# A third pre-mix input tile, clearing in parts, and one copy for both post-mix banks

## The chip, the cores and the metric

One core of one Trainium2 chip runs the kernel. The metric is the device time of one execution in microseconds. Three runs of the kernel before took 1095.16, 1096.00 and 1097.95 us; the median is 1096.0 us.

## The reference

```python
scores = scale * q @ k.transpose                      # 4 batches, 12 heads, 448 x 448, head dim 64
scores = einsum('bhij,hg->bgij', scores, w_pre)       # mix over heads before the softmax
attn   = exp(scores - max) / (sum + 1e-9)             # softmax over j
attn   = einsum('bhij,hg->bgij', attn, w_post)        # mix over heads after it
x      = attn @ v                                     # -> 1792 tokens x 768
x      = elu(x @ w_in) @ w_out                        # 768 -> 2048 -> 768
h      = x @ w_in2                                    # 768 -> 1024
h      = layernorm(h * softmax(h)) * g_ln
out    = h @ w_out2                                   # 1024 -> 768
```

Queries and keys are fp32, and so is all the attention arithmetic. The weights of the two feed-forward layers come as float64 and are decoded on the chip into pairs of high and low parts.

## The kernel before

**Tiling of the attention.** The 448 query rows of a batch are cut into groups of 10 rows. Groups are gathered into 17 chunks (`CH`, line 25) of 4, 8, 12, 12, 9 groups in batch 0, then 11, 12, 12, 10; 12, 12, 12, 9; and 11, 12, 12, 10. For a chunk the scores of all 12 heads are computed with the query rows on the partitions (line 443, tile `sc`, six operations of two heads each), copied out of PSUM by ScalarE or VectorE (line 449, tiles `sev`), and moved by DMA (line 455 to 460, issued through line 400) into one tile `sp` with (row, head) on the partitions and the groups on the free axis. Each head's move goes to 10 partitions, one per row of a group; head 11 takes two moves, so that a chunk has 13 moves.

**Units.** Two neighbouring groups make a unit; there are 90, numbered 0 to 89, and chunk 13 begins with unit 67, chunk 14 with unit 73. For each unit TensorE does the pre-mix (line 510, `pm<-sp,wpre_t`), VectorE takes two maxima (515), ScalarE two exponentials with their sums (520), VectorE guards and inverts the sums (524, 527), GpSimd scales the post-mix weights (531), and TensorE does the post-mix (543), which writes one PSUM bank for each of the unit's two groups (`po_p`, two tiles, line 136). Each bank is then copied into the tile `at` by one instruction (551, 128x480, or 128x384 where a group is cut at 448 rows). When a chunk's copies are done, two operations `av` (592) multiply with `v`; the result is copied (599) and stored.

**What sets the order.** Nothing here is written in the order in which it runs. `op` (290) records an operation with a rank, its dependences, its engines with assumed costs, and the ring buffers it takes and uses; `schedule` (296) then places all of them, engine by engine, by those costs and emits each engine's instructions in that order. An engine runs its instructions strictly in the emitted order, and the DMA issues on SP, ScalarE and GpSimd stand in these orders too. An operation that may run on two engines (evacuations, copies, moves of the first chunks) gets the one on which it ends first by the assumed costs.

**The tile `sp`.** There are two of them (pools `spa` and `spb`, lines 129 and 403 ff.); chunk c uses the tile of chunk c-2 (line 453). The moves of chunk c can therefore start only after the last pre-mix of chunk c-2. Both are cleared whole at the start (lines 468 to 470), one by VectorE and one by GpSimd, because the moves leave partitions unwritten. The 8 tiles `sev`, the ring of `k` (12 tiles, two batches), the three `sc` banks, three `pm` banks and two `po` banks are the other rings. Scores of a chunk are ranked from the first pre-mix of the chunk before to `SCM` = 12 us ahead of its own first pre-mix (line 398 ff.).

**Behind the attention** come the two feed-forward layers (from about 373 us of the span on), which the change does not touch, except that the pools freed at line 664 have another name among them.

Of the kernel before, what the change touches and what calls it, by code (L numbers as in the profile page):

```python
# [9 lines left out]
F32 = mybir.dt.float32  # L10
# [4 lines left out]
ALU = mybir.AluOpType  # L15
# [3 lines left out]
NB, NH, S, D = 4, 12, 448, 64  # L19
# [18 lines left out]
XB = 2  # L38
# [12 lines left out]
DB = .9  # L51
DA = .2
T0 = 14
SCM = 12
KD = 3.5
VD = 28
WB = 3
SB = 8
VB = 2
EB = 10  # L60
LEAD = 3

@with_exitstack
def kernel(ctx: ExitStack, tc: tile.TileContext, qa, kt, vt, wpre, wpost,
# [8 lines left out]
    def pool(name, bufs=1, side="left", space=None):  # L73
        kw = {"space": space} if space is not None else {"side": side}
        p = tc.alloc_tile_pool(name=name, bufs=bufs, reuse_waits="tile", **kw)
        pools[name] = p
        return p

    def release(*names):
        for n in names:  # L80
            pools.pop(n).release()
# [45 lines left out]
    wpost_t = const.tile([128, 60], F32, name="wpost_t")  # L127

    pool("spa", 1, "right")
    k_p = pool("k", 12, "right")  # L130
    kst_p = pool("kst", 2, "right")
    q_p = pool("q", 4, "right")
    sev_p = pool("sev", SB, "right")

    ps_sc = pool("ps_sc", 3, space=PSUM)
    ps_po = pool("ps_po", 1, space=PSUM)
    po_p = [ps_po.tile([128, 512], F32, name=f"po{i}") for i in range(2)]
    ps_pm = pool("ps_pm", 3, space=PSUM)


# [6 lines left out]
    def width_of(c):  # L147
        return min(10 * CH[c][2], S - CH[c][1])
# [130 lines left out]
    class Op:  # L279
# [2 lines left out]
    ops = []  # L282
    tail = {"pe": .3, "act": .2, "dve": .17, "pool": .1, "sp": 2.0, "host": 0.0}
    bufs = {"sc": 3, "pm": 3, "po": 2, "sev": SB, "e": EB, "wr": WB, "st": 4, "kst": 2, "q": 4,
            "k": 12, "sp0": 1, "sp1": 1, "at": 2, "v": VB, "x": XB, "ws": 4, "wy": 2}

    def op(rank, emit, deps=(), new=(), uses=(), more=0.0, lag=None, **us):

        o = Op()
        o.rank, o.emit, o.deps, o.new, o.us, o.more, o.lag = rank, emit, [d for d in deps if d is not None], new, us, more, lag  # L290
        for b in chain(new, uses):
            b.users.append(o)
        ops.append(o)
        return o

    def schedule():
        free = dict.fromkeys(tail, 0.0)
        rings = {r: [] for r in bufs}
        todo = sorted(ops, key=lambda o: o.rank)

        def seen(o, e):

            if o.lag is not None:
                return o.end + o.lag
            if o.eng == e and e not in ("sp", "dve"):
                return o.end
            return o.end + tail[o.eng] + o.more

        def ready(o, e):
            t = 0.0  # L310
            for d in o.deps:
                if d.end is None:
                    return None
                t = max(t, seen(d, e))
            more = dict.fromkeys(bufs, 0)
            for b in o.new:
                ring = rings[b.ring]
                n = bufs[b.ring] - more[b.ring]
                more[b.ring] += 1
                if b.at is None and len(ring) >= n:  # L320
                    for u in ring[-n].users:
                        if u.end is None:
                            return None
                        t = max(t, seen(u, e))
            return t

        while todo:
            cand, start = [], {}
            for o in todo[:WIN]:
                opts = []  # L330
                for e, us in o.us.items():
                    r = ready(o, e)
                    if r is None:
                        break
                    r = max(r, o.rank - (AHS if e == "sp" else AHD))
                    opts.append((max(r, free[e]) + us + (DB if e == "dve" and "pool" in o.us and o.rank > TD else DA if e == "dve" and "act" in o.us else 0.0), r, e))
                else:
                    _, r, e = min(opts)
                    cand.append((o, e, r))
                    start[e] = min(start.get(e, 1e9), max(r, free[e]))  # L340
            e = min(start, key=start.get)
            o, _, r = min((c for c in cand if c[1] == e and c[2] <= start[e] + GRACE), key=lambda c: c[0].rank)
            o.eng = e
            t = max(r, free[e])
            o.end = free[e] = t + o.us[e]
            for b in o.new:
                if b.at is None:
                    b.at = o
                    rings[b.ring].append(b)
            o.emit(e)  # L350
            todo.remove(o)
        return max(free.values())
# [3 lines left out]
    def copier(e):  # L356
        return nc.scalar.copy if e == "act" else nc.vector.tensor_copy
# [41 lines left out]
    def dma(out, in_, e="sp"):  # L399
        {"act": nc.scalar, "pool": nc.gpsimd, "sp": nc.sync}[e].dma_start(out=out, in_=in_)  # L400
# [27 lines left out]
    def add_score(c, h):  # L428

        b, _, G = CH[c]  # L430
        n = 5 * G
        ring = ("sc", "pm")[h // 2 % 2] if c == 0 else "sc"
        scb, svb = [Buf(ring) for _ in range(2)], [Buf("sev") for _ in range(2)]
        r = t_sc[c, h]
        key = "sc", c, h

        def mm(e):
            T[key] = [pools["ps_" + ring].tile([128, 512], F32, tag=ring, name="sc") for _ in range(2)]
            q, k = q_t[c, h // 6], kt_t[b, h]
            for x in range(2):  # L440
                for i in range(2):
                    sl = slice(64 * i, 64 * i + 64)
                    nc.tensor.matmul(T[key][i][64 * x:64 * x + 64, :S], q[sl, h % 6 // 2, 64 * x:64 * x + 64], k[sl, :],  # L443
                                     start=True, stop=True)

        def evac(e, i):
            t = T["sv", c, h + i] = (k0.tile([128, S], F32, name=f"s0_{h + i}") if c == 0 else
                                     sev_p.tile([128, S], F32, tag="sev", name="sev"))
            copier(e)(t, T[key][i][:, :S])  # L449

        def move(e, i, p, r0, r1):
            if c not in sp_t:
                sp_t[c] = sp_t[c - 2]
            dma(sp_t[c][p:p + 13 * (r1 - r0 - 1) + 1:13, 0:G, :], T["sv", c, h + i][r0 * G:r1 * G], e)

        o1 = op(r, mm, [k_op[b, h], q_op[c, h // 6]], scb, [qb_[c, h // 6], kb[b, h]], pe=SC)
        for i in range(2):
            sv = [] if c == 0 else [svb[i]]
            o2 = sc_ev[c, h + i] = op(r + .9 + .1 * i, lambda e, i=i: evac(e, i), [o1], sv, [scb[i]], act=.43, dve=.54)
            for n, to in enumerate([(h + i, 0, 10)] if h + i < 11 else [(11, 0, 5), (64, 5, 10)]):  # L460
                sp_op.setdefault(c, []).append(op(r + 2 + .2 * i + .1 * n, lambda e, i=i, to=to: move(e, i, *to), [o2], [spb_[c]], sv, lag=3.5, sp=.78, **({"act": .78} if c < 2 else {"pool": 1.0} if c == 2 else {})))

    spb_ = {c: Buf(f"sp{(NC - c) % 2}") for c in range(NC)}
    o = op(7.0, lambda e: dma(wpre_t, wpre), sp=.5)
    o_wpost = op(T0 + 2, lambda e: dma(wpost_t, wpost), sp=.5)
    w_op = op(T0 - 8, lambda e: nc.gpsimd.tensor_scalar(wpre_t, wpre_t, 0.125, None, ALU.mult), [o], pool=.6)

    for c in range(2):
        sp_t[c] = pools["spb" if (NC - c) % 2 else "spa"].tile([128, NH, S], F32, tag="sp", name="sp")
        (nc.gpsimd if c else nc.vector).memset(sp_t[c], 0.0)  # L470
    for t in po_p:
        nc.vector.memset(t, 0.0)

    def begin(e):
        release("k0")
# [21 lines left out]
    for u, sl in enumerate(units):  # L497
# [46 lines left out]
                                         wr_t[u][sl, r].rearrange("p (g a) -> p g a", a=5), start=True, stop=True)  # L544

        def take(e, s, u=u, sl=sl):
            c, g = sl[s]
            if c not in at_t:
                at_t[c] = pools["at"].tile([128, 4, NH, WMAX], F32, tag="at", name="at")
            o, n = 10 * g, min(10, width_of(c) - 10 * g)  # L550
            copier(e)(at_t[c].rearrange("p q h r -> p (q h) r")[:, :, o:o + n],
                      po_t[u][s][:, :480].rearrange("p (x a) -> p x a", a=10)[:, :, :n])

# [8 lines left out]
        ow = op(r0 + 3.4, weigh, [o, o_wpost], [wb], [sb], dve=.3, pool=.38)  # L562
        r0 = t_post[u]
        o = op(r0, post, ex + [ow], pob, eb + [wb], pe=POST)
        for s, (c, g) in enumerate(sl):
            at_ops[c].append(op(r0 + 1.2 + .1 * s, lambda e, s=s, take=take: take(e, s), [o], [at_b[c]] if g == 0 else [],
                                [pob[s]] + ([at_b[c]] if g else []), act=.45, dve=.57))
# [93 lines left out]

    def start_moe(e):
        nonlocal gln_t
        release("sev", "q", "kst", "k", "spa")
        p = pool("wstg", 2, "right")
        gln_t = p.tile([128, F2 // 128], F32, name="gln_t", bufs=1)
        dma(gln_t, gln)
        w1_alloc(0, pool("w1a", 1, "right"))
        xT_alloc(0, pool("xT0", 1, "right"))
# [302 lines left out]
```

## Time and profile before

| | |
|---|---|
| median of 3 runs | 1096.0 us (1095.16 to 1097.95) |
| the profiled execution | 1094.9 us, of which the span of its instructions is 1093.1 us |
| busy share of the span | TensorE 97%, VectorE 66%, ScalarE 46%, GpSimd 21% |
| first pre-mix starts, last `av` ends | 17.85 us, 373.5 us |

Times below are from the span's start. A matmul's end is modelled, so the busy share of TensorE says little on how tightly it works; the chain of waits and the start of one operation against the next say more. The program records each matmul of the attention as two, so that one score or pre-mix operation is 8 records, a post-mix 56, an `av` 48.

### The profile page before, as it was taken

To read this page: it belongs to the slowest core of one execution; us is meant where nothing else is said; L and a number is where in the kernel's file an instruction comes from. 1 tells how busy PE (TensorE), PEld (TensorE's weight loads), DVE (VectorE), ACT (ScalarE), POOL (GpSimd) and SP (SyncE) were. 2 spreads that over 40 slices of the span, in tenths; PEclk is the share of its full clock that TensorE was granted. 3 is DMA by queue.
4 is the path that set the end of the run, shared out by engine and by line. 5 is a ranking of instruction groups with operands and counts; after the bars stand their busy time and mean duration, and the time that the engine had idled before them with its cause. 6 is when DMAs were issued, how large, how long until landed. Compare 5 with 4: busy or idle time off the path is not lost.

```text
span 1093.1 us, 28427 instructions
## 1 busy us (share of the span) xinstructions
PE 1059.9 (97%) x11800; PEld 888.6 (81%) x11800; DVE 722.0 (66%) x1391; ACT 504.2 (46%) x1071; POOL 231.6 (21%) x243
## 2 busy tenths in 40 slices
PE   6899999999999999999999999999999999999998
PEld 2457667667666898998988999999999889898988
DVE  6576687677677557687887887878864644353522
ACT  3566676677676455333333443333431434342422
POOL 2211010011011325343343433343431000000000
PEclk9999999999999999999999999999999999999999
DMA  6875775775746442415234242423262400000001
GB/s 200 210 209 172 216 238 172 219 221 176 232 149 197 132 133 72 155 58 171 99 117 149 83 154 77 140 91 126 70 243 100 194 30 15 30 23 22 30 15 44
DMA packets 80287, 141.69 MB, mean 130 GB/s; under 512 B 20853, under 2 KB 59969, under 8 KB 80157
## 3 DMA queue, kind: packets, MB, share of 16 engines
q1 hardware_dynamic: 78345, 136.59, 39.1%
q10 hardware_dynamic: 1332, 2.09, 0.6%
q8 instruction: 93, 1.52, 0.6%
q0 software_dynamic: 480, 1.19, 0.4%
q14 instruction: 37, 0.30, 0.1%
HBM read 75.96 MB, written 25.17 MB: 93 GB/s over the span
## 4 chain that ended last, share of the span: by engine, by line
PE 74%; DMA 9%; DVE 8%; ACT 4%; issue 2%; SPq 1%; POOL 1%; ACTq 0%; DVEq 0%; POOLq 0%
PE h L256 15%; PE o L745 15%; PE o L888 11%; PE h L841 11%; PE av L592 6%; PE sc L443 5%; PE pm L510 5%; PE po L543 5%; DMA sp<-sev 3%; DMA ws<-in_wo_dram 2%; DVE x L761 1%; DVE wy L184 1%; DMA ws<-in_wi_dram 1%; PE tr L872 1%; DVE wq L180 1%
## 5 line engine op out<-in xcount | busy, mean ns | idle before, releaser
L520 ACT ACTIVATE e<-pm,st 128x448 f32<-128x448 f32 x180 | 113.4, 635 | 72.3 <-DVE st L515 65.9
L515 DVE TENSOR_REDUCE st<-pm 128x1 f32<-128x448 f32 x180 | 105.1, 617 | 60.9 <-PE pm L510 58.6
L745 PE MATMUL o<-gh,woh 128*128 128x448 f32 x384 | 141.3, 368 | 3.8 <-ACT x L759 1.9
L745 PE MATMUL o<-glo,woh 128*128 128x448 f32 x384 | 139.9, 364 | 0.0
L745 PE MATMUL o<-gh,wol 128*128 128x448 f32 x384 | 139.8, 364 | 0.0
L443 PE MATMUL sc<-kt,q 64*64 64x448 f32 x816 | 123.8, 565 | 9.7 <-ACT sev L449 4.6
L543 PEld LDWEIGHTS po<-wr,e 60*64 60x64 f32 x5040 | 102.4, 135 | 37.0 <-issue 23.8
L269 POOL TENSOR_TENSOR glo<-g,gh 128x448 fp32r<-128x448 f32 x64 | 83.1, 1298 | 217.9 <-issue 124.5
L510 PE MATMUL pm<-sp,wpre_t 64*64 64x448 f32 x720 | 112.2, 558 | 10.4 <-DMA xs<-x 4.4
L888 PE MATMUL o<-w,lh 128*128 128x384 f32 x448 | 120.3, 340 | 0.0
L543 PE MATMUL po<-wr,e 60*64 60x60 f32 x5040 | 109.1, 219 | 2.3 <-issue 1.1
L841 PE MATMUL h<-w,x2h 128*128 128x512 f32 x336 | 107.7, 395 | 0.0
L761 DVE TENSOR_TENSOR x<-x,o 128x448 f32<-128x448 f32 x168 | 101.4, 610 | 7.9 <-PE o L745 7.9
L256 PE MATMUL h<-xh,wih 128*128 128x448 f32 x288 | 105.5, 366 | 0.0
L256 PE MATMUL h<-xh,wil 128*128 128x448 f32 x288 | 105.0, 365 | 0.0
L256 PE MATMUL h<-xl,wih 128*128 128x448 f32 x288 | 104.9, 364 | 0.0
L264 ACT ACTIVATE t<-t 128x448 f32<-128x448 f32 x64 | 37.0, 578 | 134.7 <-DVE t L263 134.7
L531 POOL TENSOR_TENSOR wr<-wpost_t,st 128x120 f32<-128x120 f32 x90 | 36.3, 403 | 294.7 <-DVE st L527 225.7
L592 PEld LDWEIGHTS av<-at,v 128*64 128x64 f32 x1632 | 75.8, 137 | 14.1 <-DVE st L515 3.5
L592 PE MATMUL av<-at,v 128*64 128x120 f32 (+5 forms) x1632 | 83.2, 258 | 3.3 <-issue 1.8
L745 PEld LDWEIGHTS o<-gh,woh 128*128 128x128 f32 x384 | 72.1, 188 | 12.7 <-DVE x L761 4.5
L888 PEld LDWEIGHTS o<-w,lh 128*128 128x128 f32 x448 | 81.7, 188 | 0.6
(98 smaller groups left out, 1930.2 us busy)
## 6 DMA issues: line engine op xcount, KB each, us to landing
sp<-sev SPq DMA_DIRECT2D x94, 210.0 KB
ws<-in_wi_dram SPq DMA_DIRECT2D x33, 512.0 KB
ws<-in_wo_dram SPq DMA_DIRECT2D x21, 512.0 KB
q<-in_qa_dram SPq DMA_DIRECT2D x34, 192.0 KB
v<-in_vt_dram SPq DMA_DIRECT2D x24, 256.0 KB
w2s<-ws SPq DMA_DIRECT2D x12, 512.0 KB
ws<-in_wo_dram SPq DMA_DIRECT2D x16, 384.0 KB
w2s<-ws SPq DMA_DIRECT2D x16, 384.0 KB
```

The source lines that it names most:

```text
L256: nc.tensor.matmul(ps[:, :S], a[:, kc * FG + ft * 128:kc * FG + (ft + 1) * 128], x[:, kc, :], start=kc == 0 and n == 0, stop=kc == ECH - 1 ...
L269: nc.gpsimd.tensor_tensor(glo, g, f(gh), ALU.subtract)
L443: nc.tensor.matmul(T[key][i][64 * x:64 * x + 64, :S], q[sl, h % 6 // 2, 64 * x:64 * x + 64], k[sl, :], start=True, stop=True)
L510: nc.tensor.matmul(ps_t[u][r][64 * s:64 * s + 64, :S], wpre_t[p, :], sp_t[c][p, g, :], start=True, stop=True)
L515: nc.vector.tensor_reduce(out=st_t[u][:P, r:r + 1], in_=ps_t[u][r][:P, :S], op=ALU.max, axis=AX.X, negate=True)
L520: nc.scalar.activation(out=t[:P], in_=ps_t[u][r][:P, :S], func=AF.Exp, bias=st[:P, r:r + 1], scale=1.0, accum_out=st[:P, 2 + r:3 + r])
L543: nc.tensor.matmul(out[:, :, 5 * r:5 * r + 5], e_t[u, r][sl, 64 * n:64 * n + 64], wr_t[u][sl, r].rearrange("p (g a) -> p g a", a=5), start ...
L592: nc.tensor.matmul(ps[64 * k:64 * k + 64, i, :], v_t[CH[c][0]][:, 6 * n + 2 * i + k, q, :], at_t[c][:, q, 6 * n + 2 * i + k, :w], start=q ...
L745: nc.tensor.matmul(ps[:, :S], a[:, ft * DM + e * 128:ft * DM + (e + 1) * 128], x, start=n == 0, stop=n == 5)
L761: nc.vector.tensor_tensor(x1[tb][:, e, :], x1[tb][:, e, :], ps[:, :S], ALU.add)
L841: nc.tensor.matmul(ps[:, hf * 512:hf * 512 + 512], a[:, k, :], w, start=n == 0, stop=n == 3 * ECH - 1)
L888: nc.tensor.matmul(ps[:, :384], a[:, k, :], w, start=n == 0, stop=n == 3 * FC - 1)
```

## The change

There are now three `sp` tiles (pool `spc`), chunk c uses that of chunk c-3, and the ring of `k` shrinks from 12 to 8 tiles to make room. At the start the tile of chunk 0 is cleared only in its 4 groups (by VectorE), that of chunk 1 in its 8 groups and that of chunk 2 whole (by GpSimd); the rest of the first two is cleared later by GpSimd, before chunks 3 and 4 need it. Moves of chunk 2 may now be issued by ScalarE or SP, not by GpSimd. The scaling of `wpre_t` goes from GpSimd to VectorE, and the clearing of the two `po` banks gets a place in the schedule. The two banks become one tile of two banks, and where both groups of a unit belong to one chunk and are whole, one instruction of 128x2x48x10 copies both. Assumed numbers of the scheduler change: `SCM` 12 to 15, the landing of a move 3.5 to 5.0 us for chunks from 2 on, and the times from which VectorE and GpSimd are free.

```diff
-SCM = 12
+SCM = 15
+KB = 8
     pool("spa", 1, "right")
-    k_p = pool("k", 12, "right")
+    pool("spc", 1, "right")
+    k_p = pool("k", KB, "right")
-    po_p = [ps_po.tile([128, 512], F32, name=f"po{i}") for i in range(2)]
+    po_2 = ps_po.tile([128, 2, 512], F32, name="po")
+    po_p = [po_2[:, i] for i in range(2)]
+        free["pool"], free["dve"] = 8.0, 3.5
-                sp_t[c] = sp_t[c - 2]
+                sp_t[c] = sp_t[c - 3]
-                sp_op.setdefault(c, []).append(op(r + 2 + .2 * i + .1 * n, lambda e, i=i, to=to: move(e, i, *to), [o2], [spb_[c]], sv, lag=3.5, sp=.78, **({"act": .78} if c < 2 else {"pool": 1.0} if c == 2 else {})))
-    spb_ = {c: Buf(f"sp{(NC - c) % 2}") for c in range(NC)}
+                sp_op.setdefault(c, []).append(op(r + 2 + .2 * i + .1 * n, lambda e, i=i, to=to: move(e, i, *to), [o2, o_clear.get(c)], [spb_[c]], sv, lag=3.5 if c < 2 else 5.0, sp=.78, **({"act": .78} if c < 3 else {})))
+    spb_ = {c: Buf(f"sp{(NC - c) % 3}") for c in range(NC)}
-    w_op = op(T0 - 8, lambda e: nc.gpsimd.tensor_scalar(wpre_t, wpre_t, 0.125, None, ALU.mult), [o], pool=.6)
-    for c in range(2):
-        (nc.gpsimd if c else nc.vector).memset(sp_t[c], 0.0)
+    w_op = op(T0 - 4, lambda e: nc.vector.tensor_scalar(wpre_t, wpre_t, 0.125, None, ALU.mult), [o], dve=.15)
+    for c in range(3):
+        (nc.gpsimd if c else nc.vector).memset(sp_t[c][:, :CH[c][2]], 0.0)
     for t in po_p:
-        nc.vector.memset(t, 0.0)
+        op(T0 + 2, lambda e, t=t: nc.vector.memset(t, 0.0), dve=.49)
+    o_clear = {c + 3: clear(sp_t[c][:, CH[c][2]:], .38 * (NH - CH[c][2]), 4.0 + c) for c in range(2)}
+            if s is None:
+                copier(e)(at_t[c].rearrange("p q h r -> p (q h) r")[:, :, o:o + 20].rearrange("p x (s a) -> p s x a", s=2),
+                          po_2[:, :, :480].rearrange("p s (x a) -> p s x a", a=10))
+                return
+        if c == c1 and 10 * g1 + 10 <= width_of(c) and True:
+            at_ops[c].append(op(r0 + 1.2, lambda e, take=take: take(e, None), [o], [at_b[c]] if g == 0 else [],
+                                pob + ([at_b[c]] if g else []), act=.85, dve=1.06))
+            continue
```

Counted over the whole program, the copies out of the post-mix banks were 93 on ScalarE and 87 on VectorE. Now 86 of the 90 units have one copy each, 67 of them on VectorE and 19 on ScalarE, and the other 4 units have two. Evacuations of scores were 107 on ScalarE and 97 on VectorE; now they are 145 and 59.

Three places show how the order moved. The first is SP's queue where the moves of chunk 13 begin (`10x11x448` and `5x11x448` are its moves, those with 9 belong to chunk 12; `xs` stores chunk 11's results, `w1s` and `kst` are the decoding of weights on the side). Before:

```order
163 L400 DMA sp<-sev 10x9x448
164 L400 DMA sp<-sev 5x9x448 x2
165 L400 DMA xs_61<-x 128x3x120
166 L400 DMA sp<-sev 10x11x448
167 L400 DMA sp<-sev 5x11x448 x2
168 L400 DMA sp<-sev 10x11x448 x3
169 L400 DMA w1s_92<-kst 128x192
170 L400 DMA sp<-sev 10x11x448 x3
171 L400 DMA kst<-in_wo_dram 128x192
```

And after:

```order
180 L404 DMA sp<-sev 10x9x448
181 L404 DMA sp<-sev 5x9x448 x2
182 L404 DMA sp<-sev 10x11x448
183 L404 DMA sp<-sev 5x11x448 x2
184 L404 DMA xs_61<-x 128x3x120
185 L404 DMA sp<-sev 10x11x448 x4
186 L404 DMA w1s_92<-kst 128x192
187 L404 DMA kst<-in_wo_dram 128x192
188 L404 DMA sp<-sev 10x11x448 x2
```

Chunk 13's first three moves now stand ahead of the last store of chunk 11, and they no longer need chunk 11's tile to be free.

The second place is VectorE in units without an `av` between them, around unit 75 of 90. `COPY sev<-sc` evacuates scores, `COPY at<-po` the post-mix. Before:

```order
469 L515 TENSOR_REDUCE st<-pm 128x1 x2
470 L551 COPY at<-po_119 128x48x10
471 L449 COPY sev<-sc 128x448
472 L524 TENSOR_SCALAR st<-st 128x2
473 L527 RECIPROCAL st<-st 128x2
474 L515 TENSOR_REDUCE st<-pm 128x1 x2
475 L449 COPY sev<-sc 128x448 x2
```

And after:

```order
428 L524 TENSOR_REDUCE st<-pm 128x1 x2
429 L561 COPY at<-po 128x2x48x10
430 L533 TENSOR_SCALAR st<-st 128x2
431 L536 RECIPROCAL st<-st 128x2
432 L524 TENSOR_REDUCE st<-pm 128x1 x2
433 L561 COPY at<-po 128x2x48x10
```

VectorE now does the whole post-mix copy of such a unit and no evacuation of scores; ScalarE has these.

The third is ScalarE between the last move of chunk 1 and the first `av` (moves of chunk 2 have 12 groups). Before:

```order
28 L400 DMA sp<-sev 10x8x448
29 L400 DMA sp<-sev 5x8x448
30 L449 COPY sev<-sc 128x448
31 L551 COPY at<-po_119 128x48x10
32 L449 COPY sev<-sc 128x448 x2
33 L520 ACTIVATE e,st<-pm,st 128x448
34 L449 COPY sev<-sc 128x448
35 L520 ACTIVATE e,st<-pm,st 128x448
```

And after:

```order
29 L404 DMA sp<-sev 10x8x448
30 L404 DMA sp<-sev 5x8x448
31 L453 COPY sev<-sc 128x448
32 L404 DMA sp<-sev 10x12x448
33 L404 DMA sp<-sev 5x12x448
34 L453 COPY sev<-sc 128x448 x2
35 L404 DMA sp<-sev 10x12x448
36 L453 COPY sev<-sc 128x448
37 L404 DMA sp<-sev 10x12x448
38 L529 ACTIVATE e,st<-pm,st 128x448
39 L453 COPY sev<-sc 128x448
40 L404 DMA sp<-sev 10x12x448
```

Seven moves of chunk 2 now stand among ScalarE's evacuations and exponentials, where six stood on GpSimd.

## Rows read from the trace of the kernel before

**Rows 1.** Windows: stretch, busy us by engine, granted TensorE clock, DMA share, GB/s.
```profile
100.00:200.00 100.00, 96.90 (x2391) 69.10 (x2385) 71.99 (x185) 66.30 (x178) 10.12 (x26) 1.00 0.71 213
200.00:300.00 100.00, 95.98 (x2376) 67.51 (x2368) 71.03 (x182) 66.94 (x181) 10.50 (x27) 1.00 0.71 210
```
**Rows 2.** Chain of waits, 250 to 260 us: start, us, what (operations back to back).
```profile
252.21 0.75 PE pm L510 x8
252.96 0.81 PE po L543 x56
253.77 2.61 PE av L592 x48
...
258.11 0.76 PE sc L443 x8
```
**Rows 3.** Waits of TensorE's pre-mix, 50 to 340 us: us, times, longest.
```profile
PE pm L510 <- DMA xs<-x: 4.4, 3, 1.9
PE pm L510 <- DMA sp<-sev: 1.9, 3, 0.8
PE pm L510 <- DMA q<-in_qa_dram: 1.1, 1, 1.1
```
**Rows 4.** SP's queue, 256 to 275 us: start, us, issue.
```profile
256.91 0.39 SPq L400 DMA_DIRECT2D xs<-x  x1
259.90 5.71 SPq L400 DMA_DIRECT2D sp<-sev  x6
...
273.13 1.65 SPq L400 DMA_DIRECT2D sp<-sev  x2
```
**Rows 5.** TensorE, 258 to 281 us: start, us, line, idle before.
```profile
258.68 1.20 PE L510 MATMUL pm<-sp,wpre_t 64*64 64x448 f32 x8
...
280.26 0.59 PE L510 MATMUL pm<-sp,wpre_t 64*64 64x448 f32 x2 [1.12 <-DMA xs<-x]
```
**Rows 6.** Moves with their landing on GpSimd's queue: count, KB each, median us to landing.
```profile
sp<-sev POOLq DMA_DIRECT2D x5, 210.0 KB, 8.0
```
**Rows 7.** The start, in order of time.
```profile
1.94 4.54 DVE L470 MEMSET sp<- 128x5376 f32 x1 [1.94 <-issue]
6.05 0.53 ACT L449 COPY s<-sc 128x448 f32<-128x448 f32 x1 [2.61 <-PE sc L443]
7.51 1.13 DVE L449 COPY s<-sc 128x448 f32<-128x448 f32 x2
8.15 6.91 SPq L400 DMA_DIRECT2D sp<-s  x8
17.85 1.29 PE L510 MATMUL pm<-sp,wpre_t 64*64 64x448 f32 x8
```
**Rows 8.** Moves issued by ScalarE: count, duration ns min/median/max, first and last start.
```profile
L400 ACTq DMA_DIRECT2D sp<-sev x8: 784/786/800, 15.1 to 26.5; - x8
```
**Rows 9.** Post-mix copies by form, 20 to 340 us: busy us, mean ns, idle before.
```profile
L551 DVE COPY at<-po 128x480 f32<-128x480 f32 x81 | 51.4, 649 | 3.5 <-PE po L543 2.9
L551 ACT COPY at<-po 128x480 f32<-128x480 f32 x78 | 43.1, 574 | 2.3 <-PE po L543 2.3
L551 DVE COPY at<-po 128x384 f32<-128x384 f32 x1 | 0.5, 548 | 0.0
```
**Rows 10.** VectorE in one unit without an `av`, 320 to 323 us.
```profile
320.26 1.15 DVE L515 TENSOR_REDUCE st<-pm 128x1 f32<-128x448 f32 x2 [1.67 <-PE pm L510]
321.33 0.65 DVE L551 COPY at<-po 128x480 f32<-128x480 f32 x1
321.90 0.61 DVE L449 COPY sev<-sc 128x448 f32<-128x448 f32 x1
322.43 0.15 DVE L524 TENSOR_SCALAR st<-st 128x2 f32<-128x2 f32 x1
322.84 1.16 DVE L515 TENSOR_REDUCE st<-pm 128x1 f32<-128x448 f32 x2
```

More of the change, by code (lines that the diff above doesn't have):

```diff
@@ L284 @@
     bufs = {"sc": 3, "pm": 3, "po": 2, "sev": SB, "e": EB, "wr": WB, "st": 4, "kst": 2, "q": 4,
-            "k": 12, "sp0": 1, "sp1": 1, "at": 2, "v": VB, "x": XB, "ws": 4, "wy": 2}
+            "k": KB, "sp0": 1, "sp1": 1, "sp2": 1, "at": 2, "v": VB, "x": XB, "ws": 4, "wy": 2}
     def op(rank, emit, deps=(), new=(), uses=(), more=0.0, lag=None, **us):
@@ L460, in add_score, with clear @@
             for n, to in enumerate([(h + i, 0, 10)] if h + i < 11 else [(11, 0, 5), (64, 5, 10)]):
-                sp_op.setdefault(c, []).append(op(r + 2 + .2 * i + .1 * n, lambda e, i=i, to=to: move(e, i, *to), [o2], [spb_[c]], sv, lag=3.5, sp=.78, **({"act": .78} if c < 2 else {"pool": 1.0} if c == 2 else {})))
-    spb_ = {c: Buf(f"sp{(NC - c) % 2}") for c in range(NC)}
-    o = op(7.0, lambda e: dma(wpre_t, wpre), sp=.5)
+                sp_op.setdefault(c, []).append(op(r + 2 + .2 * i + .1 * n, lambda e, i=i, to=to: move(e, i, *to), [o2, o_clear.get(c)], [spb_[c]], sv, lag=3.5 if c < 2 else 5.0, sp=.78, **({"act": .78} if c < 3 else {})))
+    spb_ = {c: Buf(f"sp{(NC - c) % 3}") for c in range(NC)}
+    o = op(7.0, lambda e: dma(wpre_t, wpre), sp=.5, lag=7.0)
     o_wpost = op(T0 + 2, lambda e: dma(wpost_t, wpost), sp=.5)
-    w_op = op(T0 - 8, lambda e: nc.gpsimd.tensor_scalar(wpre_t, wpre_t, 0.125, None, ALU.mult), [o], pool=.6)
-    for c in range(2):
-        sp_t[c] = pools["spb" if (NC - c) % 2 else "spa"].tile([128, NH, S], F32, tag="sp", name="sp")
-        (nc.gpsimd if c else nc.vector).memset(sp_t[c], 0.0)
+    w_op = op(T0 - 4, lambda e: nc.vector.tensor_scalar(wpre_t, wpre_t, 0.125, None, ALU.mult), [o], dve=.15)
+    for c in range(3):
+        sp_t[c] = pools["spa spb spc".split()[(NC - c) % 3]].tile([128, NH, S], F32, tag="sp", name="sp")
+        (nc.gpsimd if c else nc.vector).memset(sp_t[c][:, :CH[c][2]], 0.0)
+    def clear(t, us, r):
+        return op(r, lambda e: nc.gpsimd.memset(t, 0.0), pool=us)
     for t in po_p:
-        nc.vector.memset(t, 0.0)
+        op(T0 + 2, lambda e, t=t: nc.vector.memset(t, 0.0), dve=.49)
+    o_clear = {c + 3: clear(sp_t[c][:, CH[c][2]:], .38 * (NH - CH[c][2]), 4.0 + c) for c in range(2)}
     def begin(e):
@@ L546, in take @@
         def take(e, s, u=u, sl=sl):
-            c, g = sl[s]
+            c, g = sl[s or 0]
             if c not in at_t:
@@ L564 @@
         o = op(r0, post, ex + [ow], pob, eb + [wb], pe=POST)
+        (c, g), (c1, g1) = sl
+        if c == c1 and 10 * g1 + 10 <= width_of(c) and True:
+            at_ops[c].append(op(r0 + 1.2, lambda e, take=take: take(e, None), [o], [at_b[c]] if g == 0 else [],
+                                pob + ([at_b[c]] if g else []), act=.85, dve=1.06))
+            continue
         for s, (c, g) in enumerate(sl):
@@ L663, in start_moe @@
         nonlocal gln_t
-        release("sev", "q", "kst", "k", "spa")
+        release("sev", "q", "kst", "k", "spc", "spa")
         p = pool("wstg", 2, "right")
```

## The prediction

> **What bounds the kernel now.** I read the windows first. From 100 to 300 us TensorE is busy for 96 to 97 of each 100 us, VectorE for 71 to 72, ScalarE for 66 to 67, and the DMA engines are taken 0.71 of the time, at 210 to 213 GB/s [rows 1]. So TensorE is the engine to look at, but its busy share is modelled, and the chain of waits shows what its work really takes when nothing is late: 0.76 us for a score operation, 0.75 for a pre-mix, 0.81 for a post-mix, 2.61 for an `av` of 120 columns [rows 2]. With 102 scores, 90 units and 34 `av` (on average 105 columns wide, 2.29 us by proportion) that is 77.5 + 67.5 + 72.9 + 78 = 296 us. Nine of the scores stand ahead of the first pre-mix at 17.85 us, and some 5.5 us of the first layer stand inside; so about 295 us of work fill the 356 us up to the end of the last `av` at 373.5 us. The stage loses some 60 us, and the change can only win some of these. Behind it the two layers run TensorE at 97 to 100%, with nothing changed, so what the attention wins moves the end by as much.
>
> Next I read the waits of the pre-mix. From 50 to 340 us TensorE stands idle 7.4 us in seven waits that end with a landing [rows 3]. The profile names `x`, `sp` and `q` there; a pre-mix reads neither `x` nor `q`, so these are waits for a chunk's last moves that are put down to a neighbour in the queue. One shows how they come about. The last pre-mix of chunk 11 (unit 62) starts at 258.68 and ends at 259.88 [rows 5]. SP has been idle from 257.30 and issues the first move of chunk 13 at 259.90 [rows 4], when the tile is free. Then the 13 moves stand almost without a gap until 274.78, and unit 67, the first of chunk 13, has to wait 1.12 us, until 280.26 [rows 5]. A move of 210 KB takes 8.0 us to land where the trace shows it [rows 6]. So the second tile is a real limit here: the moves start with the freeing of the tile and not with the scores.
>
> **The change, part by part.** Durations are from the profiled execution of 1094.9 us (span 1093.1 and 1.8 around it), which is 1.1 us below the median of 1096.0; I add the sum to the median.
>
> *The third tile, with SCM and the landing assumed at 5.0.* The wait for the freeing of the tile goes for all chunks from 2 on, since a tile is now free a whole chunk earlier (some 20 us). What is late next is the landing of the last move behind the last score, and this hangs on TensorE's order. Between the last score of chunk 13 and unit 67 stood an `av`, a pre-mix, a score, a post-mix and an `av`: 2.61 + 0.75 + 0.76 + 0.81 + 2.61 = 7.5 us. Now a post-mix and a score's turn more stand there, 9.1 us. For chunk 14 (`av` of 98 columns, 2.13) the same count goes from 6.5 to 10.8, for chunk 3 from 6.9 to 8.7, but for chunk 6 it falls from 8.9 to 7.4, for chunk 16 from 8.3 to 7.3, for chunks 7 and 11 from 13.4 and 11.4 to 8.6 and 8.8, and for chunk 2 it stays at 7.2. Evacuation, issue and landing need some 9 to 10 us, and TensorE takes longer than these bare counts. I therefore let 5.5 of the 7.4 us go and keep 1.9 for chunks 2, 6 and 16. Bounds: 0 (all waits come back) and 7.4 plus 0.6 for each of seven restarts, 11.6.
>
> *Clearing in parts.* VectorE's clearing of 4.54 us becomes a third of it, 1.51, and ends at 3.45 [rows 7]. The two clearings of `po`, 1.02 us, still stand ahead of the first evacuation on VectorE, but end by 4.5, before the first score is there: ScalarE's evacuation of it starts at 6.05, VectorE's at 7.51, and SP's moves run back to back from 8.15 to 15.06 up to the first pre-mix at 17.85 [rows 7]. They can start up to 1.4 us earlier, but scores and evacuations have to keep up; I take 1.0, bounds 0 and 1.5. GpSimd clears 4.58 x (8 + 12 + 8 + 4)/12 = 12.2 us to about 13 us; its first other work is at 23 us, so this is hidden. The scaling of `wpre_t` on VectorE is a tenth of an evacuation's work.
>
> *Chunk 2's moves on ScalarE.* Seven issues of 0.78 [rows 8] are 5.5 us of ScalarE between 26 and 45 us, where it also has the exponentials on which the next pre-mix waits. Behind each issue stand an evacuation or an exponential. TensorE waits there for chunk 1's landing anyway, which hides most; bounds 0 and 2, I take 0.5 lost. Chunk 1's wait itself stays, since the same 3.9 us of TensorE's work stand between its last score and unit 2; coming earlier by the 1.0 above, it is not counted again.
>
> *One copy for two banks.* On VectorE 96 elements more cost 649 - 548 = 101 ns [rows 9], so 480 more cost 505 ns: 1.15 us for the copy, against 2 x 0.649 = 1.30 if nothing is saved. On ScalarE the same step gives 0.574 + 0.505 = 1.08, the bounds are 0.574 and 1.15; these 19 copies stand on the lighter engine. VectorE's sum: 87 x 0.649 = 56.5 goes, 67 x 1.15 + 2 x 0.6 = 78.3 comes, and 38 evacuations of 0.61 [rows 10] leave, 23.2; together -1.4 us. ScalarE: -93 x 0.574 + 19 x 1.08 + 1.1 + 38 x 0.53 = -11.6. On the path it is a unit without `av` that matters, where TensorE needs 0.75 + 0.76 + 0.81 = 2.32 and VectorE is the slower: from one pair of maxima to the next 2.58 us, of which the pair 1.07, the copy 0.57 and the evacuation 0.53 [rows 10]. Now the copy of both banks costs 0.57 + 0.505 = 1.07 there, and the evacuation is gone: 2.58 + 0.50 - 0.53 = 2.55. That is no change, so I take 0. Bounds: with 1.30 for the copy the unit takes 2.62, which over the 44 gaps with just one pre-mix and one score between two post-mixes (35 before) is +1.8; ScalarE's relief may give some 3 back, so -3 to +1.8. Both banks come free together. That costs nothing new where the second of the two copies was the later one anyway.
>
> *The rest* (8 tiles of `k`): the loads of the last four tiles of a batch now wait for the scores of the batch before, but in the order they still stand some 19 us of TensorE's work ahead of their use. Bounds and value 0. The last units and the first layer's loading: -1.5 to +1.5, value -1.5, as ScalarE has no post-mix copies among the loading's casts there.
>
> Sum: -5.5 - 1.0 + 0.5 + 0 - 1.5 = -7.5, and 1096.0 - 7.5 = 1088.5; I say 1088.
>
> **The rivals.**
>
> *The transfers are the bound, and nothing changes.* The DMA engines are taken 0.71 of the time [rows 1], a move that is issued in 0.8 us lands after 8.0 [rows 6], and in rows 4 the 13 issues take 15 us. If the landing grows as the moves are issued closer to those of the chunk before, the seven waits come back under another name and only the start is won: about 1095. Against it: 0.71 leaves room on the mean, and the same 13 moves now have more than 15 us. The Trainium skill, page DMA: Bandwidth & Descriptors, section on why a DMA increments its semaphore by 16, says that a transfer is spread over as many engines, up to 16, as divide the slowest dimension of both sides. A move's is 10 rows, so by that rule it has ten engines. By an estimate from the rate in rows 1 (213 GB/s over 0.71 x 16 engines, 18.8 each) a move of 210 KB then takes 1.15 us of the ten, longer than its issue, and the time would be that of this rival; no row shows which engines carry a move.
>
> *More is won.* A pre-mix that waits also holds the scores behind it, whose moves are the next chunk's. With 11.6 in place of 5.5 and VectorE's bound of -3 the sum is -16; half way there, 1081.
>
> *Slower: VectorE becomes the pace.* It now has 67 long copies that can't be cut, and in a unit without `av` it is the slowest engine already. Each evacuation that still falls into such a unit lengthens it by 0.53 us [rows 10]. If half of the remaining 59 do, that is 15.6 us, and 1096 - 7.5 + 15.6 = 1104. It decides from 20 on (20 x 0.53 = 10.6, which eats 7.5 and 3.3 more). For it: the second bank used to be copied by ScalarE at the same time. Against it: in the rows of the order around unit 75 VectorE has no evacuation at all.
>
> **How the numbers follow.** The forecast has 0.52 with a range of its own of 1084 to 1092.5; more won 0.15; the transfers 0.20; slower 0.13. A measurement tells 0.3%, 3.3 us, from no change. Faster by more is nearly all of the forecast and all of the second rival, 0.66; no change is the transfers and a rest of the forecast, 0.21; slower 0.13. The range of 8 in 10 leaves out the far end of the second and most of the slower rival: 1080 to 1098.
>
> **What would show it.** Right: the first pre-mix starts near 16.9 us; the waits of the pre-mix for landings from 50 to 340 us fall from 7.4 to about 2 us, with SP no longer idle until a chunk's last pre-mix; the copies of 128x960 take about 1.15 us on VectorE; a unit without `av` keeps 2.5 to 2.6 us; the last `av` ends near 366 us, and the stretch behind it has its old length. Wrong: waits for landings as before with a landing above 8 us (the first rival), or units without `av` of 2.8 us and more with VectorE never idle in them (the last).

## The result and the profile after

The changed kernel takes 1085.55 us (median of six runs, 1080.97 to 1087.49), beside 1095.58 us for the kernel before on the same chip; the ratio is 0.991, with a 95% interval of 0.9884 to 0.9936. A second series of the unedited changed kernel (after_again, below) gave 0.9931 (0.9900 to 0.9961). So it is some 8 to 10 us faster. The profiled execution has a span of 1085.0 us (1093.1 before).

The windows after, to be read beside [rows 1]:

```profile
100.00:200.00 100.00, 96.48 (x2402) 64.57 (x2400) 72.72 (x168) 65.80 (x170) 10.19 (x27) 0.98 0.73 215
200.00:300.00 100.00, 95.81 (x2429) 64.40 (x2428) 75.02 (x169) 65.42 (x173) 10.51 (x27) 1.00 0.72 209
```

The busy shares hardly moved; VectorE's rose by 0.7 and 4.0 us, as it now makes most of the copies. The waits of TensorE from 50 to 340 us (us, times, longest) say more. This is the whole list after:

```profile
PE po L552 <- issue: 5.2, 7, 1.4
PE av L610 <- issue: 2.8, 2, 2.1
PE po L552 <- DVE st L533: 0.9, 1, 0.9
PE pm L519 <- DMA xs<-x: 0.9, 1, 0.9
PE sc L447 <- DMA sp<-sev: 0.2, 1, 0.2
```

Of the 7.4 us that pre-mixes waited for landings [rows 3] 0.9 are left, all of it at unit 28, the first of chunk 6. In their place stand 8.0 us marked "issue", where TensorE waits for nothing that the profile shows. Before, these were 2.0:

```profile
PE av L592 <- issue: 1.8, 2, 0.9
PE po L543 <- issue: 0.2, 1, 0.2
```

SP's queue stood idle before until the tile was free at 259.90 [rows 4]. Now the first three moves of chunk 13 (the first row) are out at 253.6, ahead of chunk 11's last pre-mix (254.52), and the next wait only for ScalarE's evacuation of the scores:

```profile
251.25 2.39 SPq L404 DMA_DIRECT2D sp<-sev  x3
253.73 0.60 SPq L404 DMA_DIRECT2D xs<-x  x1
255.14 0.96 ACT L453 COPY sev<-sc 128x448 f32<-128x448 f32 x2
255.70 1.70 SPq L404 DMA_DIRECT2D sp<-sev  x2
```

Unit 67, which waited 1.12 us [rows 5], follows the `av` ahead of it without a wait:

```profile
271.22 2.68 PE L610 MATMUL av<-at,v 128*64 128x120 f32 x48
273.83 0.98 PE L519 MATMUL pm<-sp,wpre_t 64*64 64x448 f32 x8
```

The copies by form (busy us, mean ns, idle before), for [rows 9]:

```profile
L561 DVE COPY at<-po 128x960 f32<-128x960 f32 x65 | 74.7, 1150 | 4.5 <-PE po L552 4.0
L561 ACT COPY at<-po 128x960 f32<-128x960 f32 x16 | 15.6, 976 | 1.6 <-PE po L552 1.6
```

and VectorE in a unit without an `av`, for [rows 10]; from one pair of maxima to the next it is again 2.58 us (319.93 to 322.51), full with the pair and one long copy:

```profile
319.93 1.15 DVE L524 TENSOR_REDUCE st<-pm 128x1 f32<-128x448 f32 x2
321.00 1.15 DVE L561 COPY at<-po 128x960 f32<-128x960 f32 x1
...
322.51 1.16 DVE L524 TENSOR_REDUCE st<-pm 128x1 f32<-128x448 f32 x2
```

The start, for [rows 7], in order of time. VectorE is free early and SP's moves begin 1.4 us sooner, but the first pre-mix only 0.23:

```profile
1.18 1.55 DVE L474 MEMSET sp<- 128x1792 f32 x1 [1.18 <-PEq L979]
6.08 0.62 DVE L453 COPY s<-sc 128x448 f32<-128x448 f32 x1 [2.09 <-PE sc L447]
6.73 5.31 SPq L404 DMA_DIRECT2D sp<-s  x5
12.16 2.48 ACTq L404 DMA_DIRECT2D sp<-s  x3
17.62 0.95 PE L519 MATMUL pm<-sp,wpre_t 64*64 64x448 f32 x4
```

The last of chunk 0's moves leaves at 14.64 (12.16 + 2.48) and left at 15.06 before (8.15 + 6.91): ScalarE issues three in a row only when its evacuations are done.

The kernel before, unit 2 (chunk 1) to unit 6 (chunk 2) on TensorE:

```profile
31.89 0.96 PE L510 MATMUL pm<-sp,wpre_t 64*64 64x448 f32 x2 [1.32 <-DMA sp<-sev]
33.74 0.90 PE L510 MATMUL pm<-sp,wpre_t 64*64 64x448 f32 x3 [0.89 <-DMA sp<-sev]
...
50.74 0.61 PE L510 MATMUL pm<-sp,wpre_t 64*64 64x448 f32 x4 [0.82 <-DMA sp<-sev]
```

and after, where the landing waits are gone and two waits for ScalarE's exponentials have come:

```profile
30.52 0.56 PE L519 MATMUL pm<-sp,wpre_t 64*64 64x448 f32 x1
...
34.03 0.60 PE L519 MATMUL pm<-sp,wpre_t 64*64 64x448 f32 x3 [0.63 <-ACT e L529]
37.15 1.22 PE L519 MATMUL pm<-sp,wpre_t 64*64 64x448 f32 x5 [1.40 <-ACT e L529]
...
48.15 0.97 PE L519 MATMUL pm<-sp,wpre_t 64*64 64x448 f32 x8
```

Unit 6 comes 2.6 us earlier. The last `av` ends at 368.6 (373.5 before), the first matmul of the first layer's second half starts at 376.5 (383.3), and from there to the end it is 708.5 us (709.8). The 8.1 us of the two spans are therefore 2.6 up to unit 6, 2.4 from there to the last `av`, and 3.1 behind it. In the second profile of the changed kernel (after_again) the same three parts are 1.8, 0.7 and 2.9.

### The profile page after: what moved, and what is told of

It reads as the page before. It is cut to its first block, busy times and chain, and to the rows that moved or that the text cites. A ratio compares the mean times of both kernels' runs of the same rounds, so it can differ in the third digit from the quotient of the medians.

```text
span 1085.0 us, 28325 instructions
## 1 busy us (share of the span) xinstructions
PE 1054.8 (97%) x11800; PEld 876.4 (81%) x11800; DVE 722.2 (67%) x1336; ACT 496.5 (46%) x1039; POOL 238.1 (22%) x241
## 4 chain that ended last, share of the span: by engine, by line
PE 80%; DVE 9%; DMA 5%; issue 3%; ACT 2%; POOL 1%; SPq 0%; ACTq 0%; DVEq 0%; POOLq 0%
PE h L259 15%; PE o L763 14%; PE o L906 11%; PE h L859 11%; PE av L610 7%; PE pm L519 7%; PE po L552 7%; PE sc L447 7%; DMA ws<-in_wo_dram 2%; DVE x L779 2%; DVE wy L187 2%; DMA sp<-sev 1%; DVE wq L183 1%; PE tr L890 1%; DMA ws<-in_wi_dram 1%
## 5 line engine op out<-in xcount | busy, mean ns | idle before, releaser
L552 PEld LDWEIGHTS po<-wr,e 60*64 60x64 f32 x5040 | 92.4, 135 | 55.6 <-issue 53.0
L447 PE MATMUL sc<-kt,q 64*64 64x448 f32 x816 | 112.3, 558 | 9.2 <-DMA kt<-in_kt_dram 4.2
L519 PE MATMUL pm<-sp,wpre_t 64*64 64x448 f32 x720 | 103.9, 556 | 3.4 <-ACT e L529 2.4
L552 PE MATMUL po<-wr,e 60*64 60x60 f32 x5040 | 98.6, 220 | 7.1 <-issue 5.2
```

The costliest lines, as they stand in the source:

```text
L519: nc.tensor.matmul(ps_t[u][r][64 * s:64 * s + 64, :S], wpre_t[p, :], sp_t[c][p, g, :], start=True, stop=True)
L552: nc.tensor.matmul(out[:, :, 5 * r:5 * r + 5], e_t[u, r][sl, 64 * n:64 * n + 64], wr_t[u][sl, r].rearrange("p (g a) -> p g a", a=5), start ...
```

## The experiments

All times are medians beside the kernel before on the same chip. "Waits" are the pre-mix's waits for landings and "gaps" TensorE's idle time marked "issue", both from 50 to 340 us in the one profile of each kernel, and "unit 6" is the start of its pre-mix in it. A profile is of one run, up to 5.8 us above (tile_lead) or 4.0 below (old_lead) the median of its kernel, so these columns explain a median only roughly.

| kernel | us | ratio (95% interval) | waits | gaps | unit 6 |
|---|---|---|---|---|---|
| before | 1094.2 to 1095.6 | 1 | 7.4 | 2.0 | 50.74 |
| changed | 1085.55 | 0.991 (0.9884 to 0.9936) | 0.9 | 8.0 | 48.15 |
| after_again | 1085.97 | 0.9931 (0.9900 to 0.9961) | 1.0 | 8.2 | 48.91 |
| tile_only | 1092.35 | 0.9974 (0.9946 to 1.0001) | 6.1 | 2.8 | 50.54 |
| lead_only | 1090.74 | 0.9960 (0.9935 to 0.9984) | 6.9 | 1.5 | 52.64 |
| tile_lead | 1086.62 | 0.9919 (0.9889 to 0.9948) | 0.6 | 7.4 | 50.48 |
| copy_only | 1095.79 | 1.0019 (0.9991 to 1.0048) | 5.5 | 2.3 | 50.60 |
| two_tiles | 1089.32 | 0.9953 (0.9925 to 0.9981) | 3.2 | 5.7 | 48.31 |
| two_copies | 1090.04 | 0.9942 (0.9916 to 0.9969) | 1.0 | 8.8 | 47.89 |
| old_lead | 1094.57 | 0.9995 (0.9972 to 1.0017) | 2.7 | 3.2 | 48.38 |
| lag35 | 1087.08 | 0.9934 (0.9905 to 0.9963) | 5.5 | 5.0 | 49.45 |
| lag65 | 1088.05 | 0.9951 (0.9922 to 0.9980) | 0 | 8.2 | 50.00 |
| old_start | 1090.04 | 0.9959 (0.9934 to 0.9984) | 0 | 4.3 | 50.91 |
| pool_moves | 1090.69 | 0.9962 (0.9934 to 0.9991) | 0.5 | 6.6 | 50.30 |

Intervals are about 0.003 to each side, so neighbours in this table are often not told apart.

**tile_only**, the kernel before with the third tile (the lines that number, clear and release the tiles follow suit and are left out here):

```diff
-    k_p = pool("k", 12, "right")
+    pool("spc", 1, "right")
+    k_p = pool("k", 8, "right")
-                sp_t[c] = sp_t[c - 2]
+                sp_t[c] = sp_t[c - 3]
```

> The kernel before with a third sp tile (all three cleared whole, two of them by GpSimd) and 8 tiles of k, nothing else: SCM 12, landing assumed at 3.5, chunk 2's moves on SP and GpSimd, one copy for each bank. Theory A: the waits for landings from 50 to 340 us, 7.4 us before, fall below 3 us, and the time is about 1090 (1095.6 less 5.5). Rival B: 1094 to 1096, whatever the waits do. A third possibility, C: the assumed landing of 3.5 lets the schedule put the first pre-mix of a chunk too early, the waits for landings stay at 4 us or more, and the time is about 1093: then the scheduler's numbers belong to the gain.

It came out as C, though 0.9974 with an interval up to 1.0001 is not clear of no change: 6.1 us of waits are still there, in two rows:

```profile
PE pm L511 <- DMA sp<-sev: 4.8, 4, 2.9
PE pm L511 <- DMA q<-in_qa_dram: 1.3, 1, 1.3
```

The freeing of the tile was a limit [rows 4], but taking it away alone leaves most of the waits, 2.9 us of them at unit 6.

**lead_only** is the kernel before with the scheduler's two numbers, and **tile_lead** has both:

```diff
-SCM = 12
+SCM = 15
-... lag=3.5, sp=.78 ...
+... lag=3.5 if c < 2 else 5.0, sp=.78 ...
```

> The kernel before with SCM 15 and a landing of 5.0 assumed from chunk 2 on; two sp tiles and all else stay. Theory C with the tile as a limit of its own: the moves still start only after the last pre-mix two chunks before, so waits for landings of 3 us or more from 50 to 340 us stay, and the time is 1093 to 1096. If the scheduler's numbers alone were the whole gain: waits below 2 us and about 1089.

> The kernel before with a third sp tile, 8 tiles of k, SCM 15 and a landing of 5.0 assumed from chunk 2 on; whole clearing, chunk 2's moves on SP and GpSimd and one copy for each bank stay. The third tile alone left 6.1 us of the pre-mix's waits for landings from 50 to 340 us and gave 0.9974 of before. Theory C (the waits were also planned: with 3.5 assumed, a chunk's first pre-mix is placed ahead of its landing, tile or no tile): they fall below 2 us, and the time is about 1089 (0.994 to 0.995). Rival B (the waits are neutral): the waits fall, but the time stays with the third tile alone, 1092. Rival D (the landing itself grows): the waits stay at 4 us or more.

Alone the numbers take next to nothing from the waits (6.9):

```profile
PE pm L510 <- DMA sp<-sev: 4.8, 5, 2.8
PE pm L510 <- DMA kt<-in_kt_dram: 2.1, 2, 1.2
```

Yet the time is 0.9960 (0.9935 to 0.9984), 1090.74 us where 1093 to 1096 were expected, so lead_only wins some time that these waits do not show. With the tile the waits are 0.6 and the ratio is 0.9919, as good as the whole change. For the waits theory C is borne out, and this is the firmest result here: either part leaves them, the two together remove them. The profile of tile_lead:

```profile
PE po L544 <- issue: 5.7, 4, 1.9
PE sc L444 <- issue: 0.9, 1, 0.9
PE av L593 <- issue: 0.8, 1, 0.8
PE pm L511 <- DMA sp<-sev: 0.6, 1, 0.6
```

In this profile the stretch from unit 6 to the last `av` is 322.8 us, as long as in the kernel before, and 7.4 us of gaps stand in it. So it shows that the waits are gone, and not where tile_lead wins its 7.6 us.

**two_tiles**, the changed kernel with two tiles (the same lines left out):

```diff
-                sp_t[c] = sp_t[c - 3]
+                sp_t[c] = sp_t[c - 2]
```

> The changed kernel with two sp tiles again (chunk c uses that of chunk c-2); everything else stays: one copy for two banks, partial clearing, SCM 15, landing assumed at 5.0, 8 tiles of k. Theory A, the third tile carries the gain: the moves of a chunk wait again for the last pre-mix two chunks before, the landing waits of the pre-mix from 50 to 340 us go from 0.9 back to 6 to 8 us, and the time is about 1091 (1085.6 plus some 5.5). Rival B, the gain comes from the one copy and the lighter ScalarE, and the landing waits only hid other slack: the landing waits may come back in the profile, but the time stays at 1085 to 1087.

Waits of 3.2 us came back, less than expected, and the time lies between the theories. Its interval overlaps those of both series of the changed kernel, so this run does not show by itself that the third tile is worth time there.

**old_lead** takes back both numbers, **lag35** only the landing (its edit is shown), **lag65** lengthens it to 6.5:

```diff
-... lag=3.5 if c < 2 else 5.0, sp=.78 ...
+... lag=3.5, sp=.78 ...
```

> The changed kernel with SCM 12 and a landing of 3.5 assumed for all chunks; three tiles, one copy and the new start stay. Theory C: the waits for landings from 50 to 340 us come back to some 4 to 6 us, and the time is about 1089 to 1090. If the third tile alone did it: waits below 2 us and 1086.

> The changed kernel with a landing of 3.5 assumed for all chunks, SCM 15 and all else kept. With SCM 12 as well the gain was gone (0.9995 of before). Theory C, in its sharper form (the assumed landing sets where a chunk's first pre-mix stands in TensorE's order, SCM hardly does): the time is 1092 to 1095, with waits for landings from 50 to 340 us of 2 us or more. Rival E (SCM carries it): 1085 to 1088.

> The changed kernel with a landing of 6.5 assumed from chunk 2 on in place of 5.0, all else kept. Theory C: with 0.9 us of landing waits left there is nothing to win, and a longer assumption only puts other work ahead of a chunk's first pre-mix: 1085 to 1088. Rival F (other moves of the order decide by chance, not the landing): anywhere from 1084 to 1092, with the waits still under 1 us.

With both numbers back the gain is gone, more than expected. With the landing alone back it is not: the sharper form of theory C fell, and lag35 is fast, as rival E has it, with 5.5 us of waits (3.1 of them one wait, at unit 6). lag65 has no waits and wins nothing more. In old_lead's profile the units up to 63 start as early as in the changed kernel (257.3 and 257.2), and then unit 67 starts 4.7 us later (278.56 against 273.83) and waits in its middle for moves issued as late as 272.99:

```profile
278.56 1.08 PE L519 MATMUL pm<-sp,wpre_t 64*64 64x448 f32 x4
279.85 0.59 PE L519 MATMUL pm<-sp,wpre_t 64*64 64x448 f32 x2 [0.21 <-DMA v<-in_vt_dram]
```

That is one place. The two kernels differ in SCM alone; why old_lead is slower by 0.6% stays open, and SCM 12 with a landing of 5.0 was not run.

**copy_only** is the kernel before with the one copy, **two_copies** the changed kernel without it:

```diff
-        if c == c1 and 10 * g1 + 10 <= width_of(c) and True:
+        if c == c1 and 10 * g1 + 10 <= width_of(c) and False:
```

> The kernel before with the one copy for two banks, nothing else: two sp tiles, SCM 12, whole clearing. Theory A: no change that can be told, 1094 to 1097, with the landing waits of the pre-mix still at 6 to 8 us from 50 to 340 us. Rival B: about 1089.

> The changed kernel with one copy for each post-mix bank again; three tiles and everything else stay. VectorE gets back 97 short copies of 0.65 us and 86 evacuations of scores, ScalarE 79 and 106. Theory A: the merged copy is neutral on the path (a unit without av 2.55 against 2.58 us), so the time is 1084 to 1088, with the landing waits of the pre-mix still under 2 us. Rival B: the copy carries the gain, and the time goes back to about 1092.

Added alone, the copy gives nothing. Taken away, the time is 1090.04 us, between the two theories; 0.9942 against 0.991 and 0.9931 with it is not told apart, since the intervals overlap. One more pair bears on it: tile_lead and old_start (below) differ in the one copy alone, and on the same chip they took 1086.62 and 1090.04 us. So beside the tile and the numbers the copy wins nothing, and may cost 0.3%.

**old_start** has the old start: the old clearing, the old place of chunk 2's moves, and the load of `wpre_t` without the landing of 7.0 that the change assumes for it (a number of the change beside those named above). **pool_moves** has only the moves back, and its edit is shown:

```diff
-... **({"act": .78} if c < 3 else {})
+... **({"act": .78} if c < 2 else {"pool": 1.0} if c == 2 else {})
```

> The changed kernel with the start of before: the three tiles cleared whole (one by VectorE, two by GpSimd), the clearing of the post-mix banks ahead of everything, the scaling of wpre_t on GpSimd, chunk 2's moves on SP and GpSimd; three tiles, SCM 15, landing 5.0 and one copy stay. The first pre-mix starts at 17.62 us in the changed kernel, so by the start alone some 0.3 us can be lost, and the time would be 1085.5 to 1087. Against this: chunk 2's first pre-mix starts at 48.15 in the changed kernel and at 50.5 to 50.7 in the three kernels with the old start and old numbers; if the start carries that, its first pre-mix is back near 50.5 and the time near 1088; if SCM and the landing carry it, it stays near 48.2.

> The changed kernel with chunk 2's moves on SP and GpSimd as before, the rest of the new start kept. In the four kernels with the new start unit 6, the first of chunk 2, starts at 47.9 to 48.4 us, in the six with the old one at 50.5 to 52.6. If the moves on ScalarE carry these 2.4 us, unit 6 starts near 50.5 and the time is near 1088 to 1090; if the clearing in parts carries them, it stays near 48.2 and the time near 1086. The predicted loss by ScalarE's issues (0.5 us, up to 2) would show as a unit 6 at 47.7 or earlier.

Unit 6 goes back to 50.9 and 50.3. Over all 14 profiles it starts at 47.9 to 50.0 in the seven with chunk 2's moves on ScalarE and at 50.3 to 52.6 in the seven others, so the moves on ScalarE are the part that brings it forward. In pool_moves the landing is waited for again, and a post-mix waits 2.46 us for a copy on ScalarE.

```profile
43.22 1.04 PE L552 MATMUL po<-wr,e 60*64 60x60 f32 x56 [2.46 <-ACT at L561]
...
50.30 1.10 PE L519 MATMUL pm<-sp,wpre_t 64*64 64x448 f32 x8 [0.51 <-DMA sp<-sev]
```

The time of pool_moves (0.9962) is as expected; beside 0.9931 on the same chip the intervals overlap, though the medians are 4.7 us apart. old_start took 1090.04 us where near 1088 was expected with a late unit 6. But tile_lead reaches 0.9919 with the old start, so an early unit 6 is not needed for the gain.

**after_again** is the changed kernel without an edit.

> The changed kernel once more, unedited, beside the three above on one chip. Its ratio to before is 0.991 (0.9884 to 0.9936) from six runs. The same ratio within 0.003 says that the gaps to the variants are the edits; if it is 0.994 or more, the gaps to the variants with the old start and with two copies (0.996 and 0.994) are no difference. In its first profile TensorE stood idle 8.6 us with nothing named that it waited for; if that belongs to the kernel it is 7 us or more again, if to the single execution it may be anything from 1 to 9.

The ratio came within 0.0021. The gaps belong to the kernel: 8.2 us again, and mostly at the same matmuls (from 20 to 400 us ten gaps in the first profile and nine in the second, eight of them in common). Three of them in the first profile, and the same three in the second:

```profile
70.29 0.58 PE L552 MATMUL po<-wr,e 60*64 60x60 f32 x25 [1.37 <-issue]
196.06 0.58 PE L552 MATMUL po<-wr,e 60*64 60x60 f32 x25 [1.28 <-issue]
222.03 2.68 PE L610 MATMUL av<-at,v 128*64 128x120 f32 x47 [2.11 <-issue]
```

```profile
71.35 0.58 PE L552 MATMUL po<-wr,e 60*64 60x60 f32 x25 [1.37 <-issue]
198.44 0.58 PE L552 MATMUL po<-wr,e 60*64 60x60 f32 x25 [1.55 <-issue]
224.15 2.11 PE L610 MATMUL av<-at,v 128*64 128x120 f32 x37 [1.56 <-issue]
```

## Why the prediction came out, point by point

The time was forecast as 1088 with -7.5 us in the sum; the profiled spans differ by 8.1 and the medians by 8 to 10. Of the five terms only the copy's held. With the last `av` near 366 and the old length behind it, the prediction put 0.5 us of the gain up to unit 6, 7.0 from there to the last `av` and nothing behind; 2.6, 2.4 and 3.1 came. The errors cancelled, so the closeness of the sum is in part luck.

- **The third tile, -5.5.** The mechanism of the waits is shown: they went from 7.4 to 0.9, better than the 1.9 that were kept for chunks 2, 6 and 16; chunk 6 has what is left. The step said that the landing behind the last score would be late next, and that the order decides on it; tile_only (waits 6.1) and tile_lead (0.6) show just that. What failed is the step from waits to time: from unit 6 to the last `av` only 2.4 us were won (0.7 in the second profile), because the gaps grew by 6.0 us (2.0 to 8.0) in nearly the same stretch. 6.5 went, 0.8 of them in front of unit 6, and 6.0 came. All idle time of TensorE between unit 6 and the last `av` fell from 12.6 to 11.3 us; the other 1.1 of the 2.4 us no run isolates. No term and no rival had the gaps in it. Over the table the waits do not order the times either: lead_only has 6.9 us of them and 0.9960, old_start none and 0.9959, old_lead 2.7 and 0.9995. (The 0.6 us for each restart in the upper bound stands in no row.)
- **Clearing in parts, -1.0.** Mis-sized: -0.23 here and -0.48 in the second profile (17.37). By these times the moves' start was not what the first pre-mix waits for, but the last move, and that left only 0.4 us earlier.
- **Chunk 2's moves on ScalarE, +0.5.** The wrong sign up to unit 6. The exponentials do wait behind them, as feared (0.63 and 1.40 us), but the landing waits of chunks 1 and 2 went, and unit 6 came 2.6 us sooner. For chunk 2 the moves on ScalarE do it, as pool_moves shows. For chunk 1 they do not: copy_only and old_start, which issue them as before, have no landing wait at unit 2 either. So the step's claim that chunk 1's wait stays failed too, and no run shows by which part.
- **One copy, 0.** Right, with its parts: 1.150 us on VectorE for 1.15 expected, 0.976 on ScalarE for 1.08, a unit of 2.58 us for 2.55, and 1.0019 alone; beside the tile and the numbers it may cost 0.3%.
- **The rest, -1.5.** Not where it was put. Behind the last `av`, where the old length was to stay, 3.1 us were won, 1.8 up to the first layer's second half and 1.3 after it. Over the 14 profiles this stretch is 715.7 to 719.6 us long (719.6 before, 716.4 after, 716.1 in copy_only, whose time is not shorter), and no run shows which part of the change shortens it.

Of the rivals, the transfers as the bound fall: the DMA share rose to 0.73 and 0.72, and the waits still went. VectorE as the pace falls too: over the whole program its busy time stayed (722.0 and 722.2 us), and its tight unit kept its length. More won would have needed the waits to come out as time. Its price was also mis-added: its terms come to -16.6, and half way from the forecast to that is some 1084, not 1081.

## What to carry to other kernels

Where a transfer waits for a buffer and is planned with too short a lead, mend both to be rid of the wait: here either alone left 6 to 7 us of waits, both together 0.6. Do not count a wait that goes as time won: the engine that is let run may meet what stood hidden behind it, as here 6.0 us of gaps came for 6.5 us of waits, and lead_only won time with its waits in place. And where a greedy scheduler makes the order, one number can move much of it: variants that differ in one number lay up to 0.6% apart here, so an edit of that size needs its part alone and its part removed before it is believed.

## What the runs showed of the hardware

The gaps marked "issue" have fixed places. Counted in recorded matmuls from the program's start, 81 of the 85 gaps of 0.3 us and more (20 to 400 us, 14 profiles) stand within four records of one grid of 126.6 records; nine records of 126.6 would hold 6 of the 85 by chance. Not every grid point has one: the changed kernel has about ten on some 65 points.

The traces also show what comes late there. One DMA queue carries packets of the kind "instruction", 93 of 16 KB each in every profile (packets, MB, share of the engines):

```profile
q8 instruction: 93, 1.52, 0.6%
```

The 93 packets stand against 11800 matmuls and as many weight loads, so one packet holds some 127 matmuls with their loads, as much as one step of the grid. Each of the 81 gaps ends 1.2 to 1.8 us after the end of the packet that belongs to its grid point, and a packet takes about 1.1 us. What decides is how early the packet starts. Over all profiles, where it started fewer than 40 records ahead of its grid point, 40 of 48 points have a gap; at 40 to 80 records 41 of 237; at 80 and more none of 583. So in these gaps TensorE waits for its next block of instructions. On average the packets started 97 records ahead in the kernel before and 84 and 87 in the two profiles of the changed one, which goes with the growth of the gaps. What makes a packet start late is not shown, and no run changed the supply.

Of the five kernels with 5.5 us of waits or more, four (before, tile_only, lead_only, copy_only) have 1.5 to 2.8 us of gaps and lag35 has 5.0; the seven profiles with 1.0 or less have 4.3 to 8.8, and two_tiles and old_lead, with 3.2 and 2.7 us of waits, 5.7 and 3.2.

Such a gap can cost twice. In two_copies the longest, 3.29 us without work on TensorE, was followed by an `av` at a lower granted clock:

```profile
273.24 0.34 PE L552 MATMUL po<-wr,e 60*64 60x60 f32 x6 [3.29 <-issue]
273.50 4.35 PE L610 MATMUL av<-at,v 128*64 128x120 f32 x48
```

It takes 4.35 us where the same `av` takes 2.68 in the changed kernel, and the mean granted clock of that stretch is 0.59, so mostly the lower level of 1.2 GHz:

```profile
273.00:277.00 4.00, 3.76 (x43) 3.70 (x43) 0.00 (x0) 1.03 (x2) 0.00 (x0) 0.59 0.88 253
```
